# Five steps of the first block on float32r parts, and a later place for the other weight splits

## The chip, the cores and the metric

One core of a Trainium2 chip runs the whole program once. The metric is the time of that run on the device in microseconds (us). The engines named here are PE (TensorE, matrix products), DVE (VectorE), ACT (ScalarE), POOL (GpSimd) and SP, whose queue issues the DMAs. Each engine takes its instructions strictly in the order in which they stand in its own queue, and semaphores hold an instruction back until what it needs is there.

## What is computed

The program chains a block-causal attention and two two-layer networks:

```python
scores = scale * np.matmul(q, k.transpose(0, 1, 3, 2))      # 4 batches, 8 heads, 576 x 64
scores = np.where(block_i >= block_j, scores, -1000000000.0)
attn = softmax(scores); x = attn @ v                         # x: 2304 tokens x 512
h = x @ w_in;  g = np.maximum(0.01 * h, h);  x = g @ w_out   # 512 -> 2048 -> 512
h = x @ w_in2; g = h / (1 + np.exp(-h));     out = g @ w_out2
```

The weights arrive as float64 and are used at float32 accuracy.

## The kernel before, in words

The 2304 tokens are cut into six blocks of 384. The first network runs block by block, each block in sixteen **steps**: step f takes 128 of the 2048 hidden columns. Its first layer (`first_layer`) multiplies the block's x by the step's w_in into the PSUM tile h, ACT applies the leaky gate (`gate1`, tile g), and its second layer (`second_layer`) adds the product with the step's w_out into four accumulators acc. Steps are numbered on through the blocks here: step 16 is the first of the second block, step 31 its last.

Two ways of multiplying are used. In the first block (steps 0 to 15) a layer is four plain float32 matmuls (lines 1114 and 1131): a **whole** half-step. In the other blocks every operand is held as two float32r tiles, a high part and the rest, and each product is three float32r matmuls, so a layer is twelve (lines 1119 to 1121 and 1139): a **parted** half-step. For that ACT copies the high part (`copy`, L296) and DVE or POOL subtracts it (`rest`, L312); for the gated values these are ghi and glo, for the attention's x xhi and xlo.

A weight comes in halves of 128x512 (two to a step, 32 in all). `convert` turns one from float64 to float32: a load into wraw, a scaled copy on ACT (L344), the low word on ACT or DVE (L352, L354), the sign bits and a shift on DVE (L357, L361), and an addition on DVE or POOL (L366). `split_weights` later makes the two parts of each half.

The attention of block b+1 is done while block b's steps run, in **units** of up to 128 query rows: scores on PE (L833 in the second block, L838 later), row maximum, normalisation and the two f16 parts of the probabilities mostly on DVE (L845 to L874), exponential on ACT (L855), a transposing DMA, and the product with the values on PE (L896 to L898). A block's first step needs the attention of all of its tokens.

`Schedule` sets the order of every engine's queue: each task has a rank and a guess of its duration, and whenever an engine is free the ready task of lowest rank is put next. A step of block b has rank 16b+f, an attention unit of the third block (block 2) ranks from 79 to 92, a conversion from 10.5 to 21. Splits have the rank of the step of the second block that uses them, less LEAD = 2: 14 to 30, ahead of all of the third block's units. PSUM gives h one bank; the 32 weight slots of `slot1` hold first the spare tiles of the start, converted weights (wx) and queries and keys, then the parts.

Of the kernel before, what the change touches and what calls it, by code (L numbers as in the profile page):

```python
# [19 lines left out]
P = 128  # L20
# [10 lines left out]
NATIVE = 15  # L31
WARM = 11
LEAD = 2.0
# [179 lines left out]
def attn_mlp_mlp(  # L213
# [112 lines left out]
    def convert(src, f, sl, rk, load_rank, to=None):  # L326
# [64 lines left out]
    def first_weights():  # L391

        got = []
        for i in range(2 * NF):
            f, sl = i // 2, slice((i % 2) * DM, (i % 2 + 1) * DM)
            rk = CONV0 + CONV1 * f
            to = wx[f][:, sl] if f < NATIVE else None
            got.append(convert(w1, f, sl, rk, LOAD0 + 2 + 10 * i if i < 4 else rk - CONV_LOAD, to))
        return got

    def split_weights():

        hi, lo, done = w1_hi, w1_lo, w1_done
        last = None
        for i in range(2 * NF):
            f, sl = i // 2, slice((i % 2) * DM, (i % 2 + 1) * DM)
            d, t_x, users = w1_got[i]

            def parts(f=f, sl=sl):
                if f not in hi:  # L410
                    hi[f], lo[f] = slot1(), slot1()
                return hi[f][:, sl], lo[f][:, sl]

            deps = [t_x]
            for at in (2 * f, 2 * f + 1):
                j = at - len(spare) - len(kq1)
                if at < len(spare):
                    deps += x_done[0]
                elif j < 0:
                    deps += kq1_users  # L420
                else:
                    deps += [steps[j].t_g2, *done[2 * j], *done[2 * j + 1]]
            ts = split(DM, lambda d=d: d["x"], parts, deps, step_of(1, f) - LEAD + i % 2, [last] if last else [])
            last = ts[0]
            if f >= NATIVE:
                users += ts
            done.append(ts)

# [679 lines left out]
    def first_layer(s):  # L1108
        s.h = ps_h.tile([P, 512], F32, tag="h", name="h")
        h = s.h[:, : s.n]  # L1110
        if s.blk == 0:
# [4 lines left out]
        hi, lo = x_hi[s.blk], x_lo[s.blk]  # L1116
        for c in range(NC):
            sl = slice(c * P, (c + 1) * P)
            nc.tensor.matmul(h, w1_lo[s.f][:, sl], hi[:, c, : s.n], start=c == 0, stop=False)  # L1119
            nc.tensor.matmul(h, w1_hi[s.f][:, sl], lo[:, c, : s.n], start=False, stop=False)  # L1120
            nc.tensor.matmul(h, w1_hi[s.f][:, sl], hi[:, c, : s.n], start=False, stop=c == NC - 1)  # L1121

    def second_layer(s):
        if s.f == 0:
# [3 lines left out]
        if s.blk == 0:  # L1128
            w = w1_got[2 * s.f + 1][0]["x"]
            for c in range(NC):  # L1130
                nc.tensor.matmul(
                    s.acc[c][:, : s.n], w[:, c * P : (c + 1) * P], s.g, start=s.f == 0, stop=s.f == NF - 1
                )
            return
        whi, wlo = w1_hi[s.f], w1_lo[s.f]
        for c in range(NC):
            sl = slice(DM + c * P, DM + (c + 1) * P)
            for i, (a, b) in enumerate(((wlo[:, sl], s.ghi), (whi[:, sl], s.ghi), (whi[:, sl], s.glo))):
                nc.tensor.matmul(  # L1139
                    s.acc[c][:, : s.n], a, b, start=s.f == 0 and i == 0, stop=s.f == NF - 1 and i == 2  # L1140
# [13 lines left out]
    def add_step(blk, f):  # L1154
        s = Step()
        s.blk, s.f = blk, f
        s.n = n = BLOCKS[blk]
        before = steps[-1] if steps else None
# [18 lines left out]
        ready = w1_done[2 * f] if blk else [w1_got[2 * f][1]]  # L1177
        deps = [*ready, *x_done[blk], before.t_gate1 if before else None]
        s.t_g1 = in_turn(3 * NC * mm(n) if blk else NC * mm32(n), deps, rk, lambda e: first_layer(s))
# [3 lines left out]
        if blk == 0:  # L1183
            return
# [5 lines left out]
    def add_second(s):  # L1190
        rk = step_of(s.blk, s.f) + 1.5
        blk, n = s.blk, s.n
        ready = [s.t_ghi, s.t_glo, *w1_done[2 * s.f + 1]] if blk else [s.t_gate1, w1_got[2 * s.f + 1][1]]
        deps = [*ready, *(outs[-1] if s.f == 0 and outs else ())]
        s.t_g2 = in_turn(3 * NC * mm(n) if blk else NC * mm32(n), deps, rk, lambda e: second_layer(s))
        if blk == 0:
            s.g_users.append(s.t_g2)
        if s.f < NF - 1:
            return
# [350 lines left out]

    spare = [slot1(F32, "spare") for _ in range(H // 2 + H // 4 + 5)]
    kq1 = [slot1(F32, "kq1") for _ in range(2 * NF - NATIVE - len(spare))]
    wx = [slot1(F32, "wx") for _ in range(NATIVE)]
# [6 lines left out]
    w1_got = first_weights()  # L1560
    w1_hi, w1_lo, w1_done = {}, {}, []
    w2s = SecondWeights()
    base = (NBLK - 1) * NF
    for blk in range(NBLK):
        for f in range(NF):
            if (blk, f) == (1, 0):
                split_weights()
# [94 lines left out]
```

## Time and profile before

| | before |
|---|---|
| median of 3 runs | 1018.32 us (1017.8 to 1019.97) |
| the profiled execution | 1017.75 us |
| its span, first to last instruction | 1016.0 us |
| PE busy in the span | 981.6 us, 97% |
| DVE, ACT, POOL busy | 762.7, 577.2, 196.3 us |
| granted TensorE clock, mean | 0.992 of full |

The program has a start (the first block's attention, up to about 52 us), the first block's steps (to about 171 us), the second block's steps (to about 257 us), a short stretch in which no step is left and the attention of the third block is finished (to 271 us), and from there the other blocks and the second network. PE's busy time counts pipelined matmuls, so what a matmul costs is read from the distance between the starts of two groups, not from its listed duration.

### The profile page before, as it was taken

Reading aid. Unit: us, or ns where it says so; the run is one execution under the profiler, and the core shown is the slowest. Engines: PE = TensorE matmul, PEld = TensorE weight load, DVE = VectorE, ACT = ScalarE, POOL = GpSimd, SP = SyncE. Lnnn points to the kernel's source line nnn. Section 1 sums busy time; section 2 is a strip of 40 time slices with the busy share of each in tenths; the row PEclk is TensorE's granted clock in tenths of the full one; section 3 lists DMA queues with packets and bytes.
Section 4 is the critical chain, followed back from the end, with each engine's and each line's share of the span. In section 5 each row is a group of like instructions: output and inputs, shape, how many; then the busy total and the mean of one; then the engine's idle time right before and its main releaser. Section 6 shows DMA issues by size and latency. Waiting matters only on the chain.

```text
span 1016.0 us, 18148 instructions
## 1 busy us (share of the span) xinstructions
PE 981.6 (97%) x6417; PEld 862.8 (85%) x6417; DVE 762.7 (75%) x1891; ACT 577.2 (57%) x1398; POOL 196.3 (19%) x287
## 2 busy tenths in 40 slices
PE   7899999999899999999999999999999999999998
PEld 4656557999799999999999898888989889898897
DVE  6888879687978878877647999976666667666564
ACT  5886768676667666666545668643333333333332
POOL 3173438112130114112203124510000000000000
PEclk9999999999799999999999999999999999999999
DMA  8757772565664656568434445410010100000000
GB/s 266 247 148 179 193 146 71 116 147 111 143 143 117 132 134 123 114 138 191 112 62 135 145 146 176 125 43 22 22 42 1 43 1 22 22 1 22 1 22 22
DMA packets 159451, 102.64 MB, mean 101 GB/s; under 512 B 131456, under 2 KB 143744, under 8 KB 159360
## 3 DMA queue, kind: packets, MB, share of 16 engines
q1 hardware_dynamic: 159360, 101.48, 39.6%
q8 instruction: 50, 0.82, 0.3%
q14 instruction: 41, 0.34, 0.1%
HBM read 67.37 MB, written 9.44 MB: 76 GB/s over the span
## 4 chain that ended last, share of the span: by engine, by line
PE 51%; DVE 3%; DMA 2%; ACT 1%; issue 1%; POOL 0%; SPq 0%; DVEq 0%; POOLq 0%; ACTq 0%
PE h L1332 13%; PE acc L1455 11%; PE acc L1471 7%; PE h L1333 6%; PE acc L1139 6%; PE h L1119 2%; PE h L1121 2%; PE h L1120 2%; PE s L838 1%; DMA wraw<-w 1%; DMA yT<-y 1%; DMA pt<-hl 1%; PE x L896 0%; DMA kqr<-kq_l 0%; PE x L898 0%
## 5 line engine op out<-in xcount | busy, mean ns | idle before, releaser
L1139 PE MATMUL acc<-ghi,w 128*128 128x384 f32 x640 | 164.2, 337 | 1.9 <-ACT ghi L296 1.2
L1344 ACT ACTIVATE xlo<-xlo 128x256 f32<-128x256 f32 x144 | 59.6, 414 | 139.1 <-DVE xlo L1341 139.0
L1332 PE MATMUL h<-xhi,w 128*128 128x512 f32 x352 | 132.0, 398 | 0.0
L1341 DVE TENSOR_REDUCE xlo<-h 128x256 f32<-128x512 f32 x144 | 99.3, 690 | 37.1 <-PE h L1333 34.8
L1139 PEld LDWEIGHTS acc<-ghi,w 128*128 128x128 f32 x640 | 114.0, 188 | 3.3 <-ACT ghi L296 1.5
L1119 PE MATMUL h<-xhi,w 128*128 128x384 f32 x320 | 109.7, 343 | 0.3 <-ACT g L1167 0.3
L1120 PE MATMUL h<-xlo,w 128*128 128x384 f32 x320 | 107.6, 336 | 0.0
L1139 PE MATMUL acc<-glo,w 128*128 128x384 f32 x320 | 107.4, 336 | 0.2 <-DVE glo L312 0.2
L1121 PE MATMUL h<-xhi,w 128*128 128x384 f32 x320 | 107.5, 336 | 0.0
L855 ACT ACTIVATE p<-s,st 128x288 f32<-128x288 f32 (+5 forms) x144 | 73.4, 512 | 47.9 <-DVE st L847 35.2
L1333 PE MATMUL h<-xhi,w 128*128 128x256 f32 x352 | 98.9, 281 | 0.0
L312 DVE TENSOR_TENSOR g<-xlo,xhi 128x256 fp32r<-128x256 f32 x136 | 61.4, 452 | 40.0 <-ACT xhi L296 39.6
L874 DVE SCALAR_TENSOR_TENSOR hl<-p,st,hl 128x576 f16<-128x576 f32 (+6 forms) x120 | 80.4, 674 | 14.5 <-ACT hl L869 11.5
L296 ACT ACTIVATE xhi<-xlo 128x256 fp32r<-128x256 f32 x144 | 59.0, 415 | 48.8 <-PE acc L1455 29.1
L1332 PE MATMUL h<-xlo,w 128*128 128x512 f32 x224 | 85.5, 398 | 0.0
L869 ACT ACTIVATE hl<-p,st 128x576 f16<-128x576 f32 (+7 forms) x111 | 65.8, 596 | 25.9 <-DVE st L865 7.2
L896 PE MATMUL x<-pt,v 128*128 128x128 f16 (+1 forms) x432 | 70.7, 214 | 9.4 <-DMA pt<-hl 4.1
L1332 PEld LDWEIGHTS h<-xhi,w 128*128 128x128 f32 x352 | 66.3, 188 | 13.7
L1167 ACT ACTIVATE g<-h 128x384 f32<-128x384 f32 x96 | 46.6, 485 | 48.1 <-PE h L1121 44.8
L897 PE MATMUL x<-pt,v 128*128 128x128 f16 (+1 forms) x432 | 68.6, 212 | 0.0
L1471 PE MATMUL acc<-w,xhi 128*128 128x512 f32 (+1 forms) x225 | 67.5, 384 | 0.0
L1333 PEld LDWEIGHTS h<-xhi,w 128*128 128x128 f32 x352 | 66.6, 189 | 1.0
(147 smaller groups left out, 2514.4 us busy)
## 6 DMA issues: line engine op xcount, KB each, us to landing
wraw<-w SPq DMA_DIRECT2D x64, 512.0 KB, 4.5
kqr<-kq_l SPq DMA_DIRECT2D x16, 480.0 KB, 4.0
v<-vL SPq DMA_DIRECT2D x32, 160.0 KB, 3.5
out<-o SPq DMA_DIRECT2D x18, 256.0 KB, 2.0
yT<-y SPq DMA_DIRECT2D x20, 192.0 KB, 2.3
kqr<-kq_l SPq DMA_DIRECT2D x8, 416.0 KB, 3.5
kqr<-kq_l SPq DMA_DIRECT2D x8, 384.0 KB, 3.5
yr<-yT SPq DMA_DIRECT2D x6, 512.0 KB, 4.0
```

The lines of the kernel that those rows point to most:

```text
L855: nc.scalar.activation(p[:rows, k0:k1], u.s[i][:rows, :w], AF.Exp, bias=nm[:rows], accum_out=s2[:rows, i : i + 1])
L874: nc.vector.scalar_tensor_tensor(hl[:rows, 1, :n], p[:rows], rc[:rows], hl[:rows, 0, :n], op0=ALU.mult, op1=ALU.subtract)
L896: nc.tensor.matmul(g.x[:, o], a, hi, start=j == 0, stop=False)
L1119: nc.tensor.matmul(h, w1_lo[s.f][:, sl], hi[:, c, : s.n], start=c == 0, stop=False)
L1120: nc.tensor.matmul(h, w1_hi[s.f][:, sl], lo[:, c, : s.n], start=False, stop=False)
L1121: nc.tensor.matmul(h, w1_hi[s.f][:, sl], hi[:, c, : s.n], start=False, stop=c == NC - 1)
L1139: nc.tensor.matmul(s.acc[c][:, : s.n], a, b, start=s.f == 0 and i == 0, stop=s.f == NF - 1 and i == 2)
L1332: nc.tensor.matmul(o, whi[:, sl], x, start=c == 0, stop=end, skip_group_check=True)
L1333: nc.tensor.matmul(o[:, :NB2], wlo[:, sl], x[:, :NB2], start=False, stop=end, skip_group_check=True)
L1341: nc.vector.tensor_reduce(place(2 * j, 2), both, axis=AX.X, op=ALU.add)
L1455: nc.tensor.matmul(o, a, b, start=bank not in seen, stop=end and j == 2, skip_group_check=True)
L1471: nc.tensor.matmul(o[:, c], a, b[:, c], start=False, stop=end, skip_group_check=True)
```

## The change

In the first block the steps are taken in another order (`order0`): hidden columns 5 to 14 first, as whole steps, then columns 0 to 4 as parted steps, then column 15 whole. So the steps numbered 10 to 14 of the program become parted. Their ten weight halves are split directly after their conversion, at the conversion's rank, and the first block's x gets its own two parts (`split_first`: high parts in the tiles xs, two operations of 128x768 on each side). The parted steps of the first block also need ghi and glo. The other 22 halves are split at the rank of their step plus 58 (LEAD = -58): 79 to 90, among the third block's attention units, no longer ahead of them. The planner's guesses for the five operations of a conversion are raised or changed, which moves its order as well.

```diff
-NATIVE = 15
+PARTED = 5
+PART_RANK = 0.0
 WARM = 11
-LEAD = 2.0
+LEAD = -58.0
@@ convert @@
-        t_y = plan.add({"ACT": act(DM)}, [t_load, *cy_free], rk, scaled, cy_after)
+        t_y = plan.add({"ACT": act(DM) + 50}, [t_load, *cy_free], rk, scaled, cy_after)
-        t_w = plan.add({"DVE": dve2x(DM), "ACT": act(DM)}, [t_load, *cc_free], rk, low, cc_after)
+        t_w = plan.add({"DVE": dve2x(DM) + 110, "ACT": act(DM) + 150}, [t_load, *cc_free], rk, low, cc_after)
-        t_c = plan.add({"DVE": dve2x(DM)}, [t_load], rk, signed, [t_w])
-        t_t = plan.add({"DVE": dve2x(DM)}, [t_y], rk, shifted)
-        t_x = plan.add(on_vector(DM), [t_w, t_c, t_t], rk, added)
+        t_c = plan.add({"DVE": dve2x(DM) + 110}, [t_load], rk, signed, [t_w])
+        t_t = plan.add({"DVE": dve2x(DM) + 60}, [t_y], rk, shifted)
+        t_x = plan.add({"DVE": dve(DM) + 70, "POOL": pool(DM)}, [t_w, t_c, t_t], rk, added)
@@ first_weights @@
+            f, sl = order0[i // 2], slice((i % 2) * DM, (i % 2 + 1) * DM)
+            rk = CONV0 + CONV1 * (i // 2)
+            to = wx[f - PARTED][:, sl] if PARTED <= f < NF - 1 else None
...
+            if f < PARTED:
+                split_weights(range(2 * f + i % 2, 2 * f + i % 2 + 1))
@@ split_weights @@
+            rk = step_of(1, f) - LEAD + i % 2
+            if f < PARTED:
+                rk = CONV0 + CONV1 * order0.index(f) + PART_RANK
+    def split_first():
...
+                hi = xs[c // 2][:, : 2 * NB0].rearrange("p (c t) -> p c t", c=2)
+                return hi, x0["lo"][:, c : c + 2, :]
+            x0_done.extend(split(2 * NB0, value, parts, t_x, CONV0 + PART_RANK))
@@ add_step @@
+        s.whole = whole = blk == 0 and s.f >= PARTED
...
+        ready = [w1_got[2 * s.f][1]] if whole else w1_done[2 * s.f]
+        if blk == 0 and not whole:
+            ready = [*ready, *x0_done]
+        s.t_g1 = in_turn(NC * mm32(n) if whole else 3 * NC * mm(n), deps, rk, lambda e: first_layer(s))
@@ at the end of attn_mlp_mlp @@
+    order0 = [*range(PARTED, NF - 1), *range(PARTED), NF - 1]
```

What the planner makes of this is seen in the queues. First ACT's queue at the gate of step 10 (the row that writes g from h), before; cy and cc from wraw are conversions, the rows with p, hl, x and xhi are attention:

```order
L1167 ACTIVATE g<-h 128x384
L869 ACTIVATE hl<-p,st 128x192
L721 ACTIVATE x_1216<-x 64x64 x2
L344 ACTIVATE cy<-wraw 128x512
L296 ACTIVATE xhi<-x_1216 128x192
L352 ACTIVATE cc<-wraw 128x512
L855 ACTIVATE p,st<-s,st 128x512
L344 ACTIVATE cy<-wraw 128x512
L352 ACTIVATE cc<-wraw 128x512
L869 ACTIVATE hl<-p,st 128x512
```

and the same place now (lines stand up to 27 further down in the changed file):

```order
L1194 ACTIVATE g<-h 128x384
L743 ACTIVATE x_1339<-x 64x64 x2
L297 ACTIVATE ghi<-g 128x384
L891 ACTIVATE hl<-p,st 128x512
L297 ACTIVATE xhi<-x_1339 128x192
L297 ACTIVATE w<-cc 128x512
L345 ACTIVATE cy<-wraw 128x512
L297 ACTIVATE w<-cc 128x512
L345 ACTIVATE cy<-wraw 128x512
L743 ACTIVATE x_1471<-x 64x128
```

Among the conversions now stand the high parts of two weight halves (w from cc) and the step's own ghi; before this place held conversions and attention alone.

Second, DVE's queue at the end of the second block, where the steps run out. Before, from behind the low gate part (glo) of step 30 to that of step 31:

```order
L727 SCALAR_TENSOR_TENSOR x_2650<-x,x_2650 64x384
L864 TENSOR_SCALAR st<-st 128x1
L865 RECIPROCAL st<-st 128x1
L312 TENSOR_TENSOR xlo<-x_2650,xhi 128x384
L312 TENSOR_TENSOR k<-kqr,k 64x384
L845 MEMSET s 64x64
L847 TENSOR_REDUCE st<-s 128x1
L871 TENSOR_SCALAR hl<-p,st 128x320
L312 TENSOR_TENSOR v<-v 128x5x64
L874 SCALAR_TENSOR_TENSOR hl<-p,st,hl 128x576
L874 SCALAR_TENSOR_TENSOR hl<-p,st,hl 128x320
L312 TENSOR_TENSOR glo<-g,ghi 128x384
```

and now, from the glo of step 31 on:

```order
L313 TENSOR_TENSOR glo<-g,ghi 128x384
L749 SCALAR_TENSOR_TENSOR x_2782<-x,x_2782 64x384
L886 TENSOR_SCALAR st<-st 128x1
L887 RECIPROCAL st<-st 128x1
L313 TENSOR_TENSOR xlo<-x_2782,xhi 128x384
L313 TENSOR_TENSOR k<-kqr,k 64x384
L867 MEMSET s 64x64
L869 TENSOR_REDUCE st<-s 128x1
L893 TENSOR_SCALAR hl<-p,st 128x320
L313 TENSOR_TENSOR v<-v 128x5x64
L896 SCALAR_TENSOR_TENSOR hl<-p,st,hl 128x576
L896 SCALAR_TENSOR_TENSOR hl<-p,st,hl 128x320
```

The same eleven rows of attention stood ahead of the last step's glo and stand behind it now: the steps have moved one place forward against the attention.

## Rows read from the trace of the kernel before

**Rows 1.** The page: span, busy time by engine, slices of a fortieth.

```profile
span 1016.0 us, 18148 instructions
...
PE 981.6 (97%) x6417; PEld 862.8 (85%) x6417; DVE 762.7 (75%) x1891; ACT 577.2 (57%) x1398; POOL 196.3 (19%) x287
...
PEclk9999999999799999999999999999999999999999
```

**Rows 2.** Busy time by stretch: length, PE, weight loads, DVE, ACT, POOL, clock, DMA.

```profile
0.00:60.00 60.00, 47.46 (x240) 30.70 (x241) 46.55 (x132) 43.16 (x112) 19.41 (x27) 0.94 0.78 250
60.00:160.00 100.00, 97.15 (x528) 58.45 (x527) 83.28 (x223) 72.15 (x176) 44.57 (x58) 1.00 0.69 158
160.00:257.00 97.00, 97.00 (x711) 89.61 (x709) 78.42 (x198) 65.59 (x155) 30.16 (x49) 1.00 0.52 109
257.00:271.00 14.00, 9.35 (x74) 7.60 (x73) 12.19 (x43) 9.81 (x29) 1.51 (x4) 0.71 0.74 159
```

**Rows 3.** PE in order of time, 160 to 177 us: start, duration, group, count.

```profile
161.96 2.83 PE L1114 MATMUL h<-x,cc 128*128 128x384 f32 x8
164.62 2.74 PE L1131 MATMUL acc<-g,wx 128*128 128x384 f32 x8
...
169.28 2.74 PE L1131 MATMUL acc<-g,cc 128*128 128x384 f32 x8
...
173.94 0.51 PE L1139 MATMUL acc<-ghi,w 128*128 128x384 f32 x2
...
176.02 0.33 PE L1119 MATMUL h<-xhi,w 128*128 128x384 f32 x1
```

**Rows 4.** DVE in order of time, 249 to 273 us.

```profile
249.55 0.55 DVE L312 TENSOR_TENSOR glo<-g,ghi 128x384 fp32r<-128x384 f32 x1
250.13 0.55 DVE L727 SCALAR_TENSOR_TENSOR x<-x,x 64x384 f32<-64x384 f32 x1
...
255.60 0.55 DVE L312 TENSOR_TENSOR glo<-g,ghi 128x384 fp32r<-128x384 f32 x1
...
272.08 0.86 DVE L312 TENSOR_TENSOR xlo<-x,xhi 128x384 fp32r<-128x384 f32 x1
```

**Rows 5.** What DVE waited for, 256 to 273 us: total, times, longest.

```profile
DVE st L862 <- ACT p L855: 0.7, 1, 0.7
DVE hl L874 <- ACT hl L869: 0.2, 1, 0.2
```

**Rows 6.** Operations by form, 160 to 271 us: busy us, mean ns, idle before.

```profile
L312 DVE TENSOR_TENSOR glo<-g,ghi 128x384 fp32r<-128x384 f32 x16 | 10.6, 661 | 2.9 <-ACT ghi L296 2.8
L312 DVE TENSOR_TENSOR w<-wx,w 128x512 fp32r<-128x512 f32 x4 | 6.2, 1562 | 0.1
L296 ACT ACTIVATE ghi<-g 128x384 fp32r<-128x384 f32 x16 | 8.3, 522 | 0.4
```

**Rows 7.** Operations by form, 60 to 160 us.

```profile
L312 DVE TENSOR_TENSOR w<-wx,w 128x512 fp32r<-128x512 f32 x7 | 5.7, 840 | 0.4 <-ACT w L296 0.4
L296 ACT ACTIVATE w<-wx 128x512 fp32r<-128x512 f32 x16 | 9.1, 622 | 0.0
L312 POOL TENSOR_TENSOR w<-wx,w 128x512 fp32r<-128x512 f32 x11 | 16.3, 1511 | 1.5 <-ACT w L296 1.5
L366 POOL TENSOR_TENSOR wx<-cy,cc 128x512 int32<-128x512 int32 x9 | 11.8, 1315 | 18.8 <-DVE cy L361 15.9 <-ACT hl L869 2.8
```

**Rows 8.** What PE waited for, 273 us to the end, the longest three.

```profile
PE x L896 <- DVE x L727: 2.5, 3, 1.1
PE x L896 <- DMA pt<-hl: 1.4, 4, 0.5
...
PE x L896 <- DVE k L312: 1.2, 1, 1.2
```

**Rows 9.** Busy time by stretch, from the first step to step 10.

```profile
51.00:127.00 76.00, 73.26 (x394) 44.08 (x394) 64.84 (x169) 56.99 (x136) 36.85 (x42) 1.00 0.69 173
```

**Rows 10.** PE in order of time: value products, and scores ahead of a whole layer.

```profile
59.08 0.22 PE L896 MATMUL x<-pt,v 128*128 128x128 f16 x1
59.13 0.22 PE L897 MATMUL x<-pt,v 128*128 128x128 f16 x1
...
73.31 1.12 PE L833 MATMUL s<-kq 64*128 64x512 f32 x2
74.36 2.85 PE L1131 MATMUL acc<-g,wx 128*128 128x384 f32 x8
...
88.59 0.48 PE L833 MATMUL s<-kq 64*128 64x128 f32 x2
89.01 2.85 PE L1131 MATMUL acc<-g,wx 128*128 128x384 f32 x8
```

More of the change, by code (lines that the diff above doesn't have):

```diff
@@ L415, in split_weights @@
             for at in (2 * f, 2 * f + 1):
-                j = at - len(spare) - len(kq1)
-                if at < len(spare):
+                j = at - n_spare - 2 - len(kq1)
+                if at < n_spare:
                     deps += x_done[0]
+                elif at < n_spare + 2:
+                    deps += [s.t_g1 for s in steps if s.blk == 0 and s.f < PARTED]
                 elif j < 0:
@@ L421, in split_weights, with value, parts @@
                 else:
[L422 to L425, printed above, removed]
+                    m = PARTED + j
+                    deps += [*[s.t_g2 for s in steps if s.blk == 0 and s.f == m], *done[2 * m], *done[2 * m + 1]]
+            rk = step_of(1, f) - LEAD + i % 2
+            if f < PARTED:
+                rk = CONV0 + CONV1 * order0.index(f) + PART_RANK
+            ts = split(DM, lambda d=d: d["x"], parts, deps, rk, [w1_last[-1]] if w1_last else [])
+            w1_last.append(ts[0])
+            if not PARTED <= f < NF - 1:
                 users += ts
             done.append(ts)
+    def split_first():
+        t_x = list(x_done[0])
+        for c in range(0, NC, 2):
+            def value(c=c):
+                return x_hi[0][:, c : c + 2, :]
+            def parts(c=c):
+                if "lo" not in x0:
+                    x0["lo"] = xp.tile([P, NC, NB], F32R, tag="xlo", name="xlo0")
+                hi = xs[c // 2][:, : 2 * NB0].rearrange("p (c t) -> p c t", c=2)
+                return hi, x0["lo"][:, c : c + 2, :]
+            x0_done.extend(split(2 * NB0, value, parts, t_x, CONV0 + PART_RANK))
     class SecondWeights:
@@ L1110, in first_layer @@
         h = s.h[:, : s.n]
-        if s.blk == 0:
+        if s.whole:
             w = w1_got[2 * s.f][0]["x"]
@@ L1127, in second_layer @@
             s.acc = s.before.acc
-        if s.blk == 0:
+        if s.whole:
             w = w1_got[2 * s.f + 1][0]["x"]
@@ L1131, in second_layer @@
                 nc.tensor.matmul(
[L1132 removed]
+                    s.acc[c][:, : s.n], w[:, c * P : (c + 1) * P], s.g, start=s.at == 0, stop=s.at == NF - 1
                 )
@@ L1139, in second_layer @@
                 nc.tensor.matmul(
-                    s.acc[c][:, : s.n], a, b, start=s.f == 0 and i == 0, stop=s.f == NF - 1 and i == 2
+                    s.acc[c][:, : s.n], a, b, start=s.at == 0 and i == 0, stop=s.at == NF - 1 and i == 2
                 )
@@ L1182, in add_step @@
         s.g_users = []
-        if blk == 0:
+        if whole:
             return
@@ L1190, in add_second @@
     def add_second(s):
-        rk = step_of(s.blk, s.f) + 1.5
+        rk = step_of(s.blk, s.at) + 1.5
         blk, n = s.blk, s.n
[L1193 to L1196, printed above, removed]
+        ready = [s.t_gate1, w1_got[2 * s.f + 1][1]] if s.whole else [s.t_ghi, s.t_glo, *w1_done[2 * s.f + 1]]
+        deps = [*ready, *(outs[-1] if s.at == 0 and outs else ())]
+        s.t_g2 = in_turn(NC * mm32(n) if s.whole else 3 * NC * mm(n), deps, rk, lambda e: second_layer(s))
+        if s.whole:
             s.g_users.append(s.t_g2)
-        if s.f < NF - 1:
+        if s.at < NF - 1:
             return
@@ L1565, in attn_mlp_mlp @@
         for f in range(NF):
+            if (blk, f) == (0, 0) and PARTED:
+                split_first()
             if (blk, f) == (1, 0):
-                split_weights()
+                split_weights(range(2 * PARTED, 2 * NF))
             add_step(blk, f)
```

41 lines of the change are left out of this document (21 added, 20 removed).

## The prediction

> **What bounds the kernel now.** I read the busy shares first [rows 1], then the table by stretch [rows 2]. PE is busy for 97% of the span, and the table says where it isn't: about 12.5 us in the first 60 us, 2.9 us from 60 to 160, nothing from 160 to 257, and 4.7 us in the 14 us from 257 to 271, where the granted clock falls to 0.71 as well. From the first step on PE is the bound, with one exception: at 257 us the steps of the second block are used up and the attention of the third isn't finished. There DVE sets the pace: it is busy for 12.2 of the 14 us, and between the gate of step 31 and the last low part of x it waits for 0.9 us in all [rows 4, 5]. So a saving on PE in the first block moves everything up to 257 us; whether it moves the third block's start depends on the attention. DVE, ACT and POOL have idle time in the first block, but not much: DVE is busy for 64.8 of the 76 us from the first step to the gate of step 10 [rows 9].
>
> **What a parted half-step saves.** From a whole second layer at 169.28 to the next parted second layer at 173.94 lie 4.66 us, which hold that layer and a parted first layer; a parted second layer takes 176.02 - 173.94 = 2.08 us [rows 3]. So a whole half-step costs 4.66 - 2.08 = 2.58 us, and from 161.96 to 164.62 a whole first layer costs 2.66 us [rows 3]. The saving is 0.50 to 0.58 us for a half, for ten halves 5.0 to 5.8 us; I take 5.4 us. No loss at the change between the two kinds of matmul is added, since the 4.66 us hold one. The Trainium skill would give more: "FP8 and Floating Point Precision", section TensorE Precision Notes, says that true float32 takes four passes, against the three products here, so a quarter of 2.58 us would go, and for ten halves the estimate is 6.4 us. The measured 2.08 us is above the 1.94 us of that rule, and the row decides.
>
> **What is added on the vector engines.** Splitting the ten halves costs what it did: they were split before as well, only later. New are the first block's x parts, 128x768 twice on ACT and twice on DVE. No row has that size. Scaled by columns from the weight's parts of 512 (ACT 622 ns, DVE 840 ns, or 1562 ns in the worse stretch) [rows 6, 7], an estimate is 1.9 us of ACT and 2.5 to 4.7 us of DVE; I take 2.5, since it falls into the earlier stretch. Five ghi and glo add 5 x 0.522 = 2.6 us of ACT and 5 x 0.661 = 3.3 us of DVE [rows 6]. This lies beside PE's work as long as these engines have idle time: DVE has 16.7 us of it from 60 to 160, 18.6 us from 160 to 257 [rows 2]. If that cover were gone, all 5.8 us of DVE would be paid; I put it at nothing, between 0 and the rival below.
>
> **The new wait.** A parted step needs, behind the addition of its weight (1.315 us on POOL), the high part (0.622 us) and the low part (1.511 us on POOL) [rows 7], so a half is ready 2.1 us later than a whole one would be. Behind a first layer that waits so stand, in PE's queue, the attention's scores and value products of the same stretch, and behind them the transposes' users on all engines. In ACT's queue the splits of the parted halves are two to four halves ahead of the step that uses them (five high parts stand before the gate of step 10, and step 11 needs the third), which is at least 2 x 2.08 us of PE's work; that covers the 2.1 us. SP issues the same 32 loads of weights, in the order of the new steps; none is added, and none has to pass another queue's work that it didn't pass before. Later splits aren't critical: 22 of 32 high parts stand ahead of the gate of step 15, and step 22 is the first that needs the thirteenth.
>
> **What the end of the second block gives back.** In the queues, the value products and scores that stand on PE before the first layer of step 31 are now exactly those that stood before step 30: 489 products and 56 score matmuls in both. DVE's queue shows the same (the eleven rows in the section on the change). So PE comes to step 31 with one more step done, 2 x 2.08 = 4.16 us, and 5.4 us less spent in the first block: 1.24 us earlier than it came to step 30. From there the same attention is left as was left from step 30, and it's DVE's: the eleven rows fill 250.13 to 255.60 without a gap worth the name [rows 4], and the rest up to 272.94 with 0.9 us of waits [rows 4, 5]. PE, which before did step 31 beside those rows, has nothing in its place. The third block so starts 5.4 - 4.16 = 1.24 us earlier, not 5.4. The bounds: 5.0 - 4.16 = 0.8 us if a half saves least; 5.8 - 4.16 = 1.6 us if most; and if DVE needs its whole 255.60 - 250.13 = 5.5 us on top of a PE that isn't early, a gain of about 0.
>
> **Start and later blocks.** Ahead of the first step, DVE has the same six conversions in the stretch of the first attention; one addition and two copies of 128x384 or more are added, one x copy goes. I take 0, with 1.5 us either way. Behind the third block's start, the queues agree again in their counts from step 33, and wholly from about step 60 to the end of the attention; between 35 and 45 the attention stands 6 to 48 value products further ahead of the steps. The waits of value products behind 273 us, 2.5 + 1.4 + 1.2 = 5.1 us [rows 8], may shrink by that; I take 0.5 us, with 2 us either way.
>
> **The sum.** 0 - 5.4 + 4.16 - 0.5 = -1.74 us. The profiled execution took 1017.75 us, so 1016.0 us on its scale. The median of the runs shown lies 0.57 us above that execution: 1016.6 us. From the bounds of the terms this case alone reaches from about 1013.5 to 1019.5.
>
> **The rivals.**
> *Gain kept.* The attention's units stand up to 48 value products ahead of the steps in places where PE waited for them, so all 5.1 us of later waits [rows 8] could go. Then -5.4 + 4.16 - 5.1 = -6.3 us: 1012.0 us on the median's scale. For it speaks that, counted over the queue with the trace's mean durations, DVE has an estimated 8 us less to do up to the third block's start, since more low parts and sums are put on POOL; against it, that these waits come one by one from single sums and transposes, and that the order is the old one again from step 60.
> *Vector-bound first block (slower).* Up to the low gate part of step 10, DVE's queue holds two attention units, four value parts, two weight parts and the two x parts more than it had done by 127 us before, and four low words and two additions less; with the mean durations of the trace that is an estimate of 8 us. PE has the units' 36 value products and two scores more there too: 36 x 0.055 us by their spacing, and two scores of 0.42 to 1.05 us [rows 10], some 3.5 us. DVE had 11.2 us idle in that stretch [rows 9]. If that idle time is all latency and can't be squeezed, PE waits for 8 - 3.5 = 4.5 us at steps 10 and 11: -1.74 + 4.5 = +2.8 us, 1021.1 us on the median's scale. It decides from the point at which DVE must be busier than 91% there (72.8 of 79.5 us); in the attention's last 14 us it came to 87% [rows 2]. The Trainium skill speaks for this rival: "SBUF — State Buffer", section Who interferes with whom, says that a DVE operation with two inputs in SBUF is held off for the whole length of a POOL operation that reads there. The low parts have that form, and the same DVE operation took 840 ns in one stretch and 1562 ns in the other [rows 6, 7], which agrees with it without proving it.
> *No effect.* The eleven rows cost their full 5.5 us and nothing is won later: -5.4 + 5.5, 1018.4 us.
>
> **How the numbers follow.** The first sum with its own bounds, half-step against returned step, gets 0.46, and most of its reach is within 0.2% (2.0 us, about what a measurement of this kernel can tell from no change): 0.20 faster, 0.25 same, 0.01 slower. Gain kept: 0.22, faster. Vector-bound: 0.21, of it 0.19 slower and 0.02 same. No effect: 0.11, same, with a tenth of it to the slower side. Together: faster 0.42, same 0.38, slower 0.20. The range goes from just below the gain kept to the vector-bound time: 1011.5 to 1021.
>
> **What would show it.** Right: the groups of parted steps in the first block at 2.08 us for each half; PE without idle time up to step 31, whose glo then starts near 249.55 - 1.24 = 248.3 us instead of 255.60; the stretch without steps longer by about 5.5 us, with DVE still over 85% busy in it and the low clock for longer; the last low part of x some 1.2 us earlier than 272.08. Wrong: PE waits in front of steps 10 to 14, released by POOL or DVE low parts of w; a third block that starts 4 us earlier or more, since then DVE's rows weren't what held it; a gain or loss that arises behind 273 us; a first step away from 52 us by over 1.5 us.

## The result, and the profile after

The changed kernel takes 1010.71 us (median of 12 runs, 1007.13 to 1015.94), the kernel before in the same sitting 1019.75 us (12 runs, 1016.18 to 1023.1). The ratio is 0.9916, 95% interval 0.9893 to 0.9939: 0.84% or some 8.6 us faster. The forecast was 1.7 us faster; the lower end of its range, 1011.5 us, lies 0.8 us above the measured median.

The first profile of the changed kernel is of the slowest of its twelve runs (1015.94 us; span 1014.2 us). So each kernel was profiled three times: spans 1016.0, 1016.8 and 1016.8 us before, 1014.2, 1006.5 and 1008.3 us after. Stages are compared over all three. The stretches of [rows 2], in that first profile of the changed kernel (length, PE, weight loads, DVE, ACT, POOL, clock, DMA):

```profile
60.00:160.00 100.00, 95.66 (x568) 65.14 (x568) 89.00 (x228) 74.15 (x181) 45.53 (x56) 0.98 0.68 168
160.00:257.00 97.00, 95.28 (x705) 88.75 (x703) 77.88 (x184) 67.46 (x160) 46.04 (x59) 1.00 0.52 108
257.00:271.00 14.00, 8.87 (x52) 7.12 (x52) 11.96 (x42) 7.97 (x24) 3.23 (x6) 0.58 0.63 132
```

PE now idles for 4.3 us from 60 to 160, where it idled for 2.9, and for 1.7 us from 160 to 257, where it didn't idle [rows 2]. The last row is as forecast: DVE busy for 85%, a lower clock.

Fixed windows shift against the work, so a second table goes by **gates**: gate k is the ACT row that writes g from h in step k. Stretches from start to gate 0, to gates 31, 32, 60, 80, 84 and to the end, the kernel before (first profile):

```profile
0.00:55.80 55.80, 43.87 (x219) 28.25 (x219) 42.38 (x126) 38.96 (x103) 15.51 (x24) 0.94 0.75 252
55.80:254.00 198.20, 194.74 (x1233) 147.53 (x1233) 162.91 (x419) 140.39 (x336) 77.42 (x106) 1.00 0.62 137
254.00:275.00 21.00, 16.35 (x121) 14.21 (x118) 18.97 (x62) 13.28 (x38) 3.59 (x8) 0.76 0.65 131
275.00:441.10 166.10, 160.93 (x1263) 153.50 (x1263) 134.87 (x401) 113.04 (x309) 34.21 (x69) 1.00 0.60 131
441.10:548.30 107.20, 105.50 (x780) 101.95 (x779) 72.04 (x174) 64.09 (x144) 24.02 (x42) 1.00 0.53 119
548.30:569.60 21.30, 18.91 (x103) 17.27 (x102) 15.43 (x32) 11.20 (x22) 2.83 (x2) 1.00 0.48 149
569.60:1016.00 446.40, 441.31 (x2713) 400.08 (x2712) 316.13 (x683) 196.24 (x452) 38.76 (x37) 1.00 0.14 47
```

The changed kernel (second profile):

```profile
0.00:48.50 48.50, 39.98 (x217) 26.23 (x218) 38.93 (x119) 37.08 (x98) 12.96 (x23) 1.00 0.78 259
48.50:244.40 195.90, 189.79 (x1248) 151.57 (x1247) 167.40 (x407) 143.06 (x343) 94.41 (x115) 1.00 0.62 142
244.40:272.80 28.40, 20.62 (x150) 17.25 (x147) 24.54 (x81) 17.53 (x49) 5.02 (x11) 0.76 0.62 124
272.80:435.80 163.00, 160.54 (x1263) 153.25 (x1261) 130.34 (x397) 110.90 (x302) 36.61 (x68) 1.00 0.61 134
435.80:540.60 104.80, 104.80 (x780) 101.74 (x777) 73.05 (x182) 63.62 (x143) 16.87 (x35) 1.00 0.55 122
540.60:557.20 16.60, 16.60 (x97) 16.60 (x96) 12.65 (x27) 9.80 (x20) 0.94 (x1) 1.00 0.55 175
557.20:1006.50 449.30, 442.73 (x2718) 400.66 (x2717) 323.35 (x691) 195.22 (x449) 40.79 (x38) 1.00 0.14 47
```

The means over three profiles each, and what the prediction comes to in the same stretches (glo of step 31 at 248.3 instead of 255.60, the third block 1.24 us earlier, 0.5 us later on):

| stretch, us | before | after | difference | forecast |
|---|---|---|---|---|
| start to gate 0 | 56.3 | 51.2 | -5.1 | 0 |
| gate 0 to 31 | 198.5 | 195.6 | -2.9 | -7.3 |
| gate 31 to 32 | 20.9 | 28.8 | +8.0 | +6.1 |
| gate 32 to 60 | 165.7 | 162.9 | -2.8 | -0.5 |
| gate 60 to 80 | 107.0 | 105.3 | -1.8 | 0 |
| gate 80 to 84 | 21.4 | 16.6 | -4.7 | 0 |
| gate 84 to the end | 446.7 | 449.2 | +2.5 | 0 |
| sum (the spans) | 1016.5 | 1009.7 | -6.9 | -1.7 |

(The executions profiled of before were a little under its medians, so these means show 6.9 us; the last digits are rounded one by one.) The surprise is in the middle: from gate 0 to gate 60 the changed kernel takes 387.3 us, before 385.1 us. Though PE has less to multiply there, nothing is won: what the parted steps save is gone by gate 60. The gain is ahead of the first step and behind step 60. The waits that went stand in the list of PE's waits from 270 to 600 us (total, times, longest). Before, 9.8 us in ten groups, the longest of them:

```profile
PE x L896 <- DVE x L727: 3.0, 4, 1.1
PE x L896 <- DMA pt<-hl: 1.4, 4, 0.5
PE acc L1139 <- ACT ghi L296: 1.2, 1, 1.2
PE x L896 <- DVE k L312: 1.2, 1, 1.2
PE s L838 <- ACT p L855: 1.0, 1, 1.0
PE acc L1139 <- DVE y L298: 0.7, 1, 0.7
```

After (second profile), 2.3 us, of which:

```profile
PE x L918 <- DMA pt<-hl: 1.1, 2, 0.8
PE s L860 <- ACT p L877: 0.6, 1, 0.6
```

### The profile page after: what moved, and what is told of

Its sections match the earlier page's. It is cut to its first block, busy times and chain, and to the rows that moved or that the text cites. A ratio compares the mean times of both kernels' runs of the same rounds, so it can differ in the third digit from the quotient of the medians.

```text
span 1014.2 us, 18266 instructions
## 1 busy us (share of the span) xinstructions
PE 982.4 (97%) x6457; PEld 872.6 (86%) x6457; DVE 770.7 (76%) x1901; ACT 576.9 (57%) x1399; POOL 205.6 (20%) x290
## 4 chain that ended last, share of the span: by engine, by line
PE 79%; DVE 11%; DMA 3%; ACT 3%; issue 2%; SPq 1%; ACTq 0%; DVEq 0%
PE acc L1165 15%; PE h L1361 12%; PE acc L1484 10%; PE acc L1500 7%; PE h L1362 6%; PE h L1145 5%; PE h L1147 5%; PE h L1146 5%; PE s L860 3%; PE h L1136 2%; PE x L918 2%; PE x L920 2%; PE x L919 2%; PE acc L1157 2%; DVE hl L896 1%
## 5 line engine op out<-in xcount | busy, mean ns | idle before, releaser
L1165 PE MATMUL acc<-ghi,w 128*128 128x384 f32 x680 | 174.6, 337 | 0.0
L1165 PEld LDWEIGHTS acc<-ghi,w 128*128 128x128 f32 x680 | 121.2, 188 | 0.7
L1146 PE MATMUL h<-xlo,w 128*128 128x384 f32 x340 | 114.5, 337 | 0.0
L1165 PE MATMUL acc<-glo,w 128*128 128x384 f32 x340 | 114.1, 336 | 0.1
L313 DVE TENSOR_TENSOR g<-xlo,xhi 128x256 fp32r<-128x256 f32 x137 | 64.1, 468 | 39.1 <-ACT xhi L297 38.7
L891 ACT ACTIVATE hl<-p,st 128x576 f16<-128x576 f32 (+6 forms) x110 | 65.0, 597 | 24.6 <-DVE st L887 13.3
L1194 ACT ACTIVATE g<-h 128x384 f32<-128x384 f32 x96 | 46.7, 486 | 56.3 <-PE h L1147 51.1
L918 PE MATMUL x<-pt,v 128*128 128x128 f16 (+1 forms) x432 | 71.6, 215 | 6.8 <-DMA pt<-hl 2.3
L1361 PEld LDWEIGHTS h<-xhi,w 128*128 128x128 f32 x352 | 66.3, 188 | 13.7
L313 DVE TENSOR_TENSOR glo<-g,ghi 128x384 fp32r<-128x384 f32 x85 | 56.3, 663 | 23.5 <-ACT ghi L297 22.8
L919 PE MATMUL x<-pt,v 128*128 128x128 f16 (+1 forms) x432 | 69.3, 213 | 0.0
L920 PE MATMUL x<-pt,v 128*128 128x128 f16 (+1 forms) x432 | 67.8, 213 | 0.0
```

The costliest lines, as they stand in the source:

```text
L313: engine[e].tensor_tensor(lo, x, hi, op=ALU.subtract)
L918: nc.tensor.matmul(g.x[:, o], a, hi, start=j == 0, stop=False)
L919: nc.tensor.matmul(g.x[:, o], hd.vb[:, j], hi, start=False, stop=False)
L1165: nc.tensor.matmul(s.acc[c][:, : s.n], a, b, start=s.at == 0 and i == 0, stop=s.at == NF - 1 and i == 2)
L1361: nc.tensor.matmul(o, whi[:, sl], x, start=c == 0, stop=end, skip_group_check=True)
```

## The experiments

Times differ by a us or two from sitting to sitting, so each run is given by its ratio to the runs of before beside it. Letters of theories hold within a run's own text.

**The changed kernel again, and two parts undone.** No edit; then `LEAD` back; then the old guesses back.

> The changed kernel once more, for a second profile and more times. Measured so far: 1010.7 us median, 7.1 to 15.9 us above 1000, and one profile of 1014.2 us span in which the third block's first step came 5 us later than before and the blocks behind it won it back. Theory A (the ten parted half-steps give their 5 us, and the long stretch without steps costs more or less by chance): a profile near the median shows the third block's start some 2 to 4 us earlier than the kernel before. Theory B (the gain arises behind 273 us, from the new order of the attention): it shows that start at or behind that of before, and the gain behind it. Ratio to before 0.990 to 0.993 under both.

> The changed kernel with LEAD = 2 again: the 22 other halves are split at the rank of their step, ahead of the third block's units; parted steps and new planner guesses stay. Theory A (parted steps pay, 5 us): 0.993 to 0.996. Theory C (the later rank of the splits pays, since DVE and POOL are free for the attention at the end of the first block): 1.000 or slower, as the vector engines then have the ten splits and the others in one go. Theory D (the new guesses for the conversions pay): 0.991 to 0.994.

```diff
-LEAD = -58.0
+LEAD = 2.0
```

> The changed kernel with the old planner guesses for the five operations of a conversion; parted steps and LEAD = -58 stay. Theory A: 0.992 to 0.996. Theory D (the new guesses pay): 0.998 to 1.002, the gain is gone. Theory C: 0.991 to 0.994.

```diff
-        t_y = plan.add({"ACT": act(DM) + 50}, [t_load, *cy_free], rk, scaled, cy_after)
+        t_y = plan.add({"ACT": act(DM)}, [t_load, *cy_free], rk, scaled, cy_after)
...
-        t_x = plan.add({"DVE": dve(DM) + 70, "POOL": pool(DM)}, [t_w, t_c, t_t], rk, added)
+        t_x = plan.add(on_vector(DM), [t_w, t_c, t_t], rk, added)
```

The three operations between them are undone likewise. Measured: 0.9925 (0.9905 to 0.9945), 0.9952 (0.9935 to 0.9969) and 1.0022 (1.0009 to 1.0036). The later rank is worth some 2.6 us, the guesses 9.5 us: with the old ones the rest of the change gains nothing (it is 0.2% slower than before). PE then idles for 6.4 us between gates 10 and 16, against 2.9 us, gate 0 stands at 55.8 us, and gates 80 to 84 take 20.4 us.

**Guesses and later rank without parted steps; guesses alone in before.**

> The kernel before with LEAD = -58 and the new planner guesses, all sixteen steps of the first block whole: everything but the parted steps. Theory A: 0.997 to 1.001, as PE has its 5 us more. Theories C and D: 0.991 to 0.996, since the gain is one of order.

> The kernel before with the new guesses and nothing else of the change. Theory G (the guesses pay by themselves, start and second network): 9 us less than before, about 1010 us, and the parted steps and the later rank are worth nothing. Theory P (guesses and parted steps pay only together, since the engines must be free enough to make the parts in time): within 2 us of before, 1017 to 1021 us. With the later rank of the splits the same kernel took 1017.7 us, so theory P is the likelier.

Both are the kernel before with the new guesses in `convert`; the first has `LEAD = -58` as well. Measured 0.9992 (0.9976 to 1.0008) and 0.9998 (0.9985 to 1.0011). Their gate 0 comes early, at 48.7 and 51.2 us, but gate 0 to gate 31 takes 206.2 and 203.7 us instead of 198.5: the early start is waited away. So the guesses don't pay without the parted steps, with the later rank or without it, and the parted steps don't pay with all guesses old; the two pay together.

**Guesses for one network's weights only.**

> The changed kernel with the new guesses for the first network's weights alone, the old ones for the second network's. With the old guesses for both it took 1021.0 us, with the new for both 1011.5. Theory W1 (the guesses pay in the start and in the first two blocks): nearly all of the 9.5 us stays, 1012 to 1014 us, and the 4.7 us between gates 80 and 84 are made up by what follows. Theory W2 (they pay where the second network's weights are converted): 1017 to 1020 us. Theory both: 4.7 us are lost between gates 80 and 84, 1016 us.

> The changed kernel with the new guesses for the second network's weights alone, the old ones for the first network's. Theory W1: 1019 to 1021 us, the first step's gate at 55 to 56 us. Theory W2: 1012 to 1014 us. Theory both: 1016 us, with the first step's gate at 55 to 56 us and the stretch from gate 80 to gate 84 at about 16.7 us instead of 21.3.

```diff
-        t_y = plan.add({"ACT": act(DM) + 50}, [t_load, *cy_free], rk, scaled, cy_after)
+        t_y = plan.add({"ACT": act(DM) + 50 * (src is w1)}, [t_load, *cy_free], rk, scaled, cy_after)
```

In the other run it is w2; the rest of `convert` goes likewise. Measured 0.9899 (0.9861 to 0.9937) and 0.9927 (0.9899 to 0.9956). Either half of the guesses keeps nearly all of the gain, and in both gates 80 to 84 take 16.7 us. So they don't pay at one place of their own: each gives another order of the queues. Against the kernel with all guesses old (e3), the first half (e6) has gate 0 at 50.9 us instead of 55.8, 4.7 us less from gate 0 to 31 and 3.7 us less from gate 80 to 84; the second half (e7) leaves the first two as they were and takes 20.3 us instead of 27.7 from gate 31 to 32, and 3.7 us less from gate 80 to 84. Both lose some 3 us again behind gate 84. Of the four orders tried, the one with all guesses old is the slow one. None of the theories had that.

**The order alone, in the kernel before.** One number: the rank of the fourth block's attention (`blk` 3).

> The kernel before with one number changed: the attention of the fourth block gets a rank lower by 24. Its matmul queue then has, from step 28 to the end of the second network's start, the same counts of value products and scores ahead of each step as the changed kernel (792 products ahead of step 44, where before had 744), without a parted step in the first block. Theory O (the waits behind 273 us went because the attention stands further ahead): PE's waits from 273 to 600 us fall from 9.6 to below 4 us, the way from gate 32 to gate 80 from 273 to 268 or 269 us; the second block's end gives back 7 us (28 us from gate 31 to gate 32); all in all 1016 to 1019 us, since the give-back is moved work and not lost where the vector engines set gate 32. Theory X (they went for another reason, such as vector work already done in the first block): gate 32 to gate 80 stays at 272 to 273 us.

```diff
-            return (blk - 1 + k / n_ticks * (ATT1 if first else ATT_SLOPE)) * NF + (ATT0 if first else ATT)
+            return (blk - 1 + k / n_ticks * (ATT1 if first else ATT_SLOPE)) * NF + (ATT0 if first else ATT if blk != 3 else ATT + (-24))
```

Measured 1.0037 (1.0019 to 1.0056), 3.8 us slower. Gate 31 to 32 and gate 32 to 60:

```profile
252.00:283.10 31.10, 22.20 (x151) 19.19 (x149) 25.05 (x83) 17.88 (x50) 5.49 (x13) 0.67 0.60 131
283.10:444.80 161.70, 160.16 (x1261) 152.91 (x1259) 130.17 (x394) 111.87 (x302) 34.09 (x67) 1.00 0.58 132
```

Gate 31 comes 2 us earlier than in before (first profile) and gate 32 8 us later; 4.4 us of that come back up to gate 60 (161.7 against 166.1 us), since the fourth block's attention stands further ahead. This is the mechanism of both stretches of the changed kernel, without a parted step: order makes the give-back and also shortens what follows. The net is a loss.

> The kernel before with the fourth block's attention ranked lower by 8: the end of the second block stays as it was (513 value products ahead of step 31), and ahead of step 44 stand 780 products instead of 744. Theory O: gate 32 stays at 275 us and gate 32 to gate 80 takes 269 to 271 us, a gain of 2 to 4 us in all. Theory X: nothing within 1.5 us.

The same edit with 8: 1.0006 (0.9985 to 1.0027). Up to step 31 PE's order stayed, but ahead of step 32 more of the fourth block's attention got in, and gate 32 came 7.3 us late all the same. Gates 32 to 80 took 269.8 us (273.3 before), and 80 to 84 16.6 us. My theory said gate 32 would stay; that was wrong. But the run shows that the wait at gates 80 to 84 goes without parted steps and with the old guesses.

> The changed kernel with the fourth block's attention ranked higher by 16: 744 value products stand ahead of step 44, as in the kernel before, and up to step 34 nothing changes. Theory O: the waits between gates 32 and 80 come back, 2 to 4 us, to 1013.5 to 1015.5 us. Theory X: 1010.5 to 1012.5 us, as the changed kernel.

The changed kernel with `ATT + 16` for the fourth block: 0.9946 (0.9924 to 0.9968). Gates 32 to 80 take 272.2 us instead of 268, nearly what before took. So the order does it, not vector work saved earlier. The stretch shows this, not the whole time, whose interval overlaps the changed kernel's.

**Seven parted steps.**

> The changed kernel with seven parted steps instead of five, fourteen half-steps instead of ten. Theory A (a parted half-step saves its 0.54 us and PE is the bound): four halves less, 2 us faster, 1009.5 us. Theory D (the splits' vector work sets gate 32, so that PE's saving is waited away in front of it): no faster, 1011 to 1014 us, with gate 32 at 275 us or later and more waits of PE in the first block.

```diff
-PARTED = 5
+PARTED = 7
```

Measured 0.9992 (0.9971 to 1.0012): all of the gain is gone. Between gates 10 and 16 PE idles for 9.3 us, and its waits from 124 to 172 us begin with:

```profile
PE h L1145 <- POOL w L313: 3.2, 1, 3.2
PE h L1145 <- ACT g L1194: 1.9, 1, 1.9
...
PE h L1145 <- DVE w L313: 0.8, 1, 0.8
```

First layers (h) wait for the low parts of their weights (w). This is the vector-bound rival, and it decides between five and seven steps; the time lies above theory D's 1011 to 1014 us (median 1019.37 us).

**Splits later still.**

> The changed kernel with the 22 later splits ranked 16 later again (LEAD = -74). Its queues are the changed kernel's up to the middle of the second block; there the attention then stands as in the kernel before: 489 value products ahead of step 30 (468 in the changed kernel) and 744 ahead of step 44 (792). So the parted steps are there and the steps have not moved forward against the attention. Theory C (what the end of the second block gives back is half won again between gates 32 and 60): gate 31 to gate 32 takes 20 to 22 us instead of 28, gate 32 to gate 60 164 to 166 us instead of 163, and what is won in the net is 3 to 5 us: 1006.5 to 1008.5 us. Theory V (the vector engines set gate 32, whatever the order): gate 32 stays at 219 to 220 us behind gate 0 as in before, gate 31 comes later instead, and the time is 1010 to 1014 us.

```diff
-LEAD = -58.0
+LEAD = -74.0
```

Measured 0.9887 (0.9851 to 0.9923); a second set of runs (e17, below) 0.9899. Gates 31 to 32 and 32 to 60:

```profile
247.80:269.60 21.80, 17.30 (x119) 15.76 (x116) 19.30 (x64) 13.28 (x37) 3.50 (x8) 0.69 0.64 125
269.60:435.00 165.40, 160.63 (x1266) 153.49 (x1266) 136.18 (x399) 112.74 (x308) 33.91 (x69) 1.00 0.58 132
```

With the attention back in its old place the give-back falls from 28.8 to 21.8 us, and the shorter stretch behind it is lost again (165.4 us). Gate 0 to gate 60 is 383.2 us here, 1.9 us under before, but 385.4 us in a second profile (e17), as before. So it is some 3 us below the changed kernel's 387.3 us; that any of the parted steps' saving arrives there isn't shown, as before takes 385.1.

> The changed kernel with the splits ranked 16 later (LEAD = -74) and the fourth block's attention ranked lower by 2: 489 value products stand ahead of step 30, as in the kernel before, and 792 ahead of step 44, as in the changed kernel. So it has both orders that looked good, each in its place. Theory I (the two are independent): gate 31 to gate 32 takes 22 us, gate 32 to gate 60 163 us, and it is 2.4 us faster than the splits-later kernel. Theory T (the 2 to 3 us that are won between gates 32 and 60 are the give-back's time, used by the vector engines for the fourth block's attention, and can't be had without it): gate 31 to gate 60 takes 187 us or more, as in the splits-later kernel, wherever the waits fall, and the times agree within 1.5 us.

> The changed kernel with LEAD = -74 once more, beside the run above and in more rounds: 1006 to 1010 us, and gate 31 to gate 60 again 187 us.

e16 adds `ATT - 2` for the fourth block. Measured 0.9894 (0.9852 to 0.9937; 1007.45 us, 1004.09 to 1008.61) and, without that, 0.9899 (0.986 to 0.9937; 1008.38 us, 1006.16 to 1010.23). Gates 31 to 32 and 32 to 60 of e16:

```profile
247.00:265.50 18.50, 13.67 (x115) 11.94 (x113) 16.46 (x55) 12.86 (x36) 3.92 (x8) 0.91 0.66 139
265.50:430.60 165.10, 160.66 (x1266) 153.89 (x1266) 134.22 (x408) 113.40 (x308) 36.03 (x70) 1.00 0.58 133
```

The stretch to gate 60 stayed at 165 us: PE idles 4.4 us in it, about as without the early attention (4.8 us in e13), only sooner: 3.2 us of it before gate 44, where e13 had 0.5. So theory I's 163 us didn't come, and the times of the two kernels agree, as theory T says. But gate 31 to gate 60 took 183.6 us, less than either theory gave, and 187.8 us in e17: between gates 31 and 32 DVE had 16.46 us of work instead of 19.30, and the granted clock was 0.91 instead of 0.69. With one execution of e16 it stays open whether the 2.8 us up to gate 60 can be had without the longer give-back. The medians of e13, e16 and e17 are the lowest of all, and their ratios lie below the changed kernel's 0.9916 to 0.9942, though the intervals overlap and e6 came to 0.9899 as well.

**Second and third profiles.**

> The kernel before once more, for a second profile of it: which of the differences to the changed kernel are there in any execution and which belong to one execution. Theory S (the new guesses bring the start forward): the gate of the first step stands again at 54 to 57 us, against 48.5 us in the second profile of the changed kernel. Theory V (the start varies from one execution to the next, in any kernel): it stands between 48 and 52 us, and the 7 us are no term of the change. The way from gate 32 to gate 95 takes 339.5 us in the first profile of before; where it takes 338 to 341 again, the 9 us that the changed kernel wins there are the change's.

> The changed kernel, for a third profile of it: its first step's gate stood at 54.8 us in one and at 48.5 us in the other, and the two spans differed by 7.7 us. Theory K (the clock that is granted in the first 56 us decides): the gate stands at 48 to 49 us if the clock is 1.00, 50 to 52.5 at 0.97, 52.5 to 55 below, and the span follows with 1006.5 + (gate - 48.5) us, give or take 2 us. Theory L (vector work sets the later gates): the span does not follow the gate.

> The kernel before, for a third profile of it: the first step's gate at 55 to 57 us as in both before, gate 31 to gate 32 21 us, gate 32 to gate 60 165 to 166 us, gate 80 to gate 84 21.3 us, if these are the kernel's and not the execution's.

Ratios 0.9979 (0.9952 to 1.0006) and 1.0004 (0.9982 to 1.0027) for before against itself, 0.9942 (0.9907 to 0.9977) for the changed kernel. Before repeats itself within 1.3 us in every stretch up to gate 84. The changed kernel's third profile has gate 0 at 50.4 us with a clock of 0.97, and a span of 1008.3 us; theory K gives 1006.5 + 1.9 = 1008.4. For the first profile it gives 1012.8 us, and the span was 1014.2. So the three spans follow their gates 0 within 1.4 us.

## Why the prediction was wrong, step by step

Two terms failed: the start, put at 0, gave 5.1 us, and the waits behind gate 32, put at 0.5 us, gave 6.8 us in the net. From gate 0 to gate 32, where 1.2 us were to be won, 5.0 us were lost (4.4 us less up to gate 31, 1.9 us more from there to gate 32). That the whole came near the rival "Gain kept" is luck in part, since these errors cancel.

**A parted half-step: right.** The distance of 2.08 us shows at once (PE in order of time, second profile):

```profile
131.08 0.51 PE L1165 MATMUL acc<-ghi,w 128*128 128x384 f32 x2
...
133.16 0.33 PE L1145 MATMUL h<-xs,w 128*128 128x384 f32 x1
```

**The start: wrong, -5.1 us for 0.** I counted conversions ahead of the first step, and the count holds; but their places among the normalisations on DVE changed. PE's wait for normalised tiles was 4.6 us before (4.2 and 4.3 in the other profiles) and is 1.0 us now, in all three; the second profile's row stands below:

```profile
PE pt L1053 <- DVE spare L1047: 4.6, 3, 2.1
```

```profile
PE pt L1075 <- DVE spare L1069: 1.0, 2, 0.7
```

Over all profiles gate 0 stood at 48.5 to 54.8 us in kernels with the new guesses for the first network (the changed one, e2, e4, e6, e8, e11 to e14, e16, e17) and at 54.7 to 57.0 us with the old ones (before, e3, e7, e9, e10). So this term belongs to the guesses, which I had called a change of order and not priced. But part of it goes with the clock. With the new guesses gate 0 stood at 48.5 to 48.7 us where the mean granted clock up to it was 1.00 (three profiles), at 50.4 to 52.1 at 0.97 (six), at 51.7 and 52.6 at 0.93 and 0.94, at 54.8 at 0.91; with the old ones the clock was 0.91 or 0.94 in all seven. At 0.93 or 0.94 alone the guesses are worth 2 to 5 us, at 0.91 some 0.3 and 1.3 us; whether their order also brings the higher clock isn't shown.

**Gate 0 to gate 31: 4.4 us less than forecast.** PE's busy time fell by 5.4 us in the mean of the three profiles (194.74 to 189.79 us in the tables above), where the forecast, with the saving and the attention moved behind step 31, needed 7.3; what keeps the other 1.9 us isn't shown. And its idle time rose from 3.1 to 5.6 us. The "nothing" at which I put the added vector work was too low: not at the place of the rival (no first layer waits for weights with five parted steps), but in the attention's scores and value products, which come later from the same engines.

**The give-back: right in kind, 1.9 us too small.** DVE's order was the forecast one, the low part of step 31 now ahead of the attention's rows (first profile, in which gate 0 is only 1 us early):

```profile
253.05 0.55 DVE L313 TENSOR_TENSOR glo<-g,ghi 128x384 fp32r<-128x384 f32 x1
253.63 0.55 DVE L749 SCALAR_TENSOR_TENSOR x<-x,x 64x384 f32<-64x384 f32 x1
...
275.55 0.86 DVE L313 TENSOR_TENSOR xlo<-x,xhi 128x384 fp32r<-128x384 f32 x1
```

Counted from gate 0, the last low part of x came at 216.3 us before (272.08 - 55.8) [rows 4], and at 216.0 and 217.4 us in the other two profiles; in the three of the changed kernel it came at 220.8, 220.0 and 218.6 us: 1.2 to 4.8 us later, not 1.2 us earlier. DVE's work in the stretch grew as forecast, by 5.6 us (18.97 to 24.54 us in the tables) against the 5.5 us of the eleven rows. What I left out are its waits: 0.7 to 0.9 us before, 2.4 us now. The longest is one for scores on PE, which before did not have there:

```profile
DVE s L867 <- PE s L860: 1.3, 2, 0.7
```

It is the same in all three profiles of the changed kernel, with a granted clock of 0.65, 0.76 and 0.65 in this stretch; some 30 matmuls that stood between gates 16 and 31 before now stand in it.

**Later waits: the step that failed most.** I priced them at 0.5 us out of the three longest groups, 5.1 us [rows 8]; up to 600 us alone there were 9.8 us of waits in ten groups. And I took the third block's start and the waits behind it as separate terms; the runs show them as tied: gates 31 to 32 and 32 to 60 take 20.9 and 165.7 us in before, 21.8 and 165.3 in e13, 28.8 and 162.9 in the changed kernel, 31.0 and 161.8 in e9, 34.6 and 159.3 in e2. While PE has no step, DVE and ACT go on with the next block's attention, and what they finish then PE doesn't wait for later. Then, "wholly the same from step 60" was read from PE's counts alone. Between gates 80 and 84 it isn't PE's order that cost 4.7 us but the order on ACT and DVE. In before, the last copy of the fifth block's sums (y from acc) stands on DVE behind the low part glo of step 81, which waits for ACT, and PE waits for the copy (0.7 us above). Later ACT has the copy of a weight, waiting 2.53 us for DVE's addition, ahead of step 82's ghi, and PE waits for that ghi (1.2 us above). DVE, then ACT:

```profile
553.73 0.56 DVE L312 TENSOR_TENSOR glo<-g,ghi 128x384 fp32r<-128x384 f32 x1 [1.00 <-ACT ghi L296]
554.21 0.55 DVE L298 COPY y<-acc 128x384 f32<-128x384 f32 x1
```

```profile
562.09 0.63 ACT L296 ACTIVATE w<-cc 128x512 fp32r<-128x512 f32 x1 [2.53 <-DVE cc L366]
562.62 0.51 ACT L296 ACTIVATE ghi<-g 128x384 fp32r<-128x384 f32 x1
```

In the changed kernel (second profile) the copy is ACT's, and ghi of step 82 stands ahead of the weight:

```profile
545.13 0.49 ACT L297 ACTIVATE y<-acc 128x384 f32<-128x384 f32 x1
...
549.77 0.53 ACT L297 ACTIVATE ghi<-g 128x384 fp32r<-128x384 f32 x1
552.12 0.63 ACT L297 ACTIVATE w<-cc 128x512 fp32r<-128x512 f32 x1 [1.83 <-DVE cc L367]
```

The stretch takes 20.4 to 21.4 us in the five profiles that have the old order at both places (before three times, e3, e9), and 16.6 to 17.3 us in all others, which have it at neither. Which of the two costs how much no run shows. DVE also waited 1.18 us for an addition on POOL there, up to 551.58, but behind that it stood idle for another 1.00 us for ghi (553.73), so that wait delayed neither row. Behind gate 84 2.5 us are lost again; why stays open.

**The rivals.** "Gain kept", 1012.0 us, is nearest to the measured 1010.71 us, and half for its reason: the attention further ahead removes waits. But the give-back, which I left standing in it, was larger, and the start and gates 80 to 84 were not in it. The vector-bound rival came true at seven parted steps. (Added up from their own lines, the chances are 0.37 for the same and 0.21 for slower, not 0.38 and 0.20.)

**What stays open:** why an early start is kept with parted steps and waited away without them (e4, e8), and which rows of the old order cost the 9.5 us of e3 beside the 3.7 us between gates 80 and 84.

## What to carry to other kernels

Price a change to a planner's guesses like a change of code: here it was worth nothing alone, and with none of it the parted steps were worth nothing. Where one engine runs out of work because another sets the pace, follow the sum two stages on, since the idle time moves with the order; and count the queues of the engines that are waited for, not only that of the busy one. Then try the rank: 16 more on `LEAD` took this kernel to 0.989 of before.

## What the runs showed of the hardware

The same kernel starts at either clock. From 10 to 15 us the first and the second profile of the changed kernel read:

```profile
10.00:15.00 5.00, 3.85 (x10) 2.37 (x10) 3.83 (x14) 3.53 (x10) 0.00 (x0) 0.51 1.05 386
```

```profile
10.00:15.00 5.00, 3.50 (x21) 2.49 (x22) 4.83 (x18) 4.26 (x12) 0.00 (x0) 1.00 1.05 389
```

In both, PE's longest wait of the start was that for the first load of queries and keys, 3.4 and 3.6 us; one execution was granted mostly the lower level (1.2 GHz) in this stretch and did 10 matmuls, the other the full 2.4 GHz and did 21. At step 0 the first profile fell to the lower level once more, behind a wait of 2.68 us (0.66 granted from 50 to 55 us), and the layer took 4.54 us instead of 2.85:

```profile
50.21 4.54 PE L1136 MATMUL h<-x,wx 128*128 128x384 f32 x8 [2.68 <-ACT x L297]
```

```profile
45.37 2.85 PE L1136 MATMUL h<-x,wx 128*128 128x384 f32 x8 [0.82 <-ACT x L297]
```

Their gates 0 lie 6.3 us apart; 1.7 us of that are this layer and 1.9 us the longer wait ahead of it. The spans followed (1014.2 and 1006.5 us), so the start accounts for most of the 7.7 us between these two executions; that it does so for the 9 us by which the twelve runs differ isn't shown.

The second fact is of DVE beside POOL. In the kernel before, around gate 80, DVE and then POOL in order of time:

```profile
544.09 0.47 DVE L357 TENSOR_SCALAR cc<-wraw 128x512 uint16<-128x512 uint16 x1
...
546.70 1.79 DVE L312 TENSOR_TENSOR xhi<-yr,xhi 128x512 fp32r<-128x512 f32 x1
548.41 1.56 DVE L357 TENSOR_SCALAR cc<-wraw 128x512 uint16<-128x512 uint16 x1
...
552.04 0.69 DVE L312 TENSOR_TENSOR w<-cc,w 128x512 fp32r<-128x512 f32 x1
```

```profile
546.43 1.50 POOL L312 TENSOR_TENSOR xlo<-yr,xlo 128x512 fp32r<-128x512 f32 x1 [0.41 <-ACT xlo L296]
547.89 1.75 POOL L312 TENSOR_TENSOR w<-cc,w 128x512 fp32r<-128x512 f32 x1
550.04 1.50 POOL L366 TENSOR_TENSOR cc<-cy,cc 128x512 int32<-128x512 int32 x1 [0.41 <-DVE cc L357]
```

The subtraction of 128x512 took 1.79 us beside POOL's and 0.69 us at 552.04, when POOL's last row had ended at 551.54. The sign operation (L357) took 1.56 us beside POOL and 0.47 us at 544.09, ahead of POOL's first row there (544.73). Both began behind a POOL operation and ended 0.56 and 0.33 us after it. This agrees with the Trainium skill, "SBUF — State Buffer", section Who interferes with whom, by which a DVE operation with two inputs in SBUF contends with a POOL operation that reads there, and the one that is issued first blocks the other. For an operation with one input, as the sign operation, the page says it of the two-port modes alone; no row shows in which mode it ran. No run here took POOL away to prove it.
